# An mLSTM cell and a gated feed-forward layer on one core: the second chunk's query load, scores and values are issued earlier

## The chip, the cores and the metric

The kernel runs on one core of a Trainium2 chip. The metric is the device time of one execution in microseconds (us), the median of the runs shown.

## The reference

The first part is an mLSTM cell over 768 time steps, for 4 batches and 8 heads of 40 features. The second part takes its output as 3072 rows of 320 numbers through two weight matrices with a gelu between them. Everything is float32.

```python
for t in range(S):
    m_new = np.maximum(f_gate[:, :, t] + m, i_gate[:, :, t])
    f_stab = np.exp(f_gate[:, :, t] + m - m_new)
    i_stab = np.exp(i_gate[:, :, t] - m_new)
    C = f_stab * C + i_stab * np.einsum('bhd,bhe->bhde', vt, kt)
    n = f_stab * n + i_stab * kt
    h_tilde = np.einsum('bhde,bhe->bhd', C, qt)
    denom = np.maximum(np.abs(np.einsum('bhd,bhd->bh', n, qt)), 1.0)
    y[:, :, t] = sigmoid(o_gate) * h_tilde / denom
h = x @ w_in                      # (3072, 320) @ (320, 2048)
g = h * sigmoid(1.702 * h)
out = g @ w_out                   # (3072, 2048) @ (2048, 320)
```

## The kernel before

The time axis is cut into six chunks of 128 steps (`w` = 0 to 5; `NW`, `L`). Inside a chunk the recurrence is done in matrix form: scores (keys by queries) times decay weights, times values, plus the queries by the state carried in from the chunk before. All 32 heads of a chunk are worked on; for chunks from the second on, in two halves of 16 heads (`c` = 0, 1).

There is no scheduler at work: the order in which the Python code calls the engines is the order of each engine's queue. The main loop runs over the chunks. For chunk `w` it first makes the product with `w_in` and the gelu (`up` in chunk 0, `up_fast` and `up_strips` later; eight steps `j`), and then the product with `w_out` (`down` in chunk 0), cut into blocks. Between the blocks stand pieces of the attention of chunk `w + 1`: `attention(w + 1)` returns a table `side` of what follows which block, by the list `at`. When the blocks are done, chunk `w + 1`'s first product needs that attention's output, transposed and split (`x_high`, `x_diff` and others).

In chunk 0 `down` is called for 16 blocks: batch `b` 0 to 3, four pieces `n` of the inner dimension, first pieces 0 and 1 of all batches, then 2 and 3. A block is four float32 products of 128 x 320, each of them two rows in the trace (L973). Block `i` stands in the order (b, n) = (0,0) (0,1) (1,0) (1,1) (2,0) (2,1) (3,0) (3,1) (0,2) (0,3) (1,2) and so on.

The steps for the second chunk (`w` = 1) that the change touches:

- `load_squares(1, "q")` (L112 to L116) loads the queries by two DMAs on SP's queue into `q_sq`, in a form from which VectorE can transpose blocks of 32 features. `fill_squares(q_sq)` (L118 to L122) moves the last 8 of the 40 features to their own rows, two copies on ScalarE. `block_transposes(1, n)` for odd `n` (L417 to L421) makes `qT` from it, four transposes on VectorE.
- `load(1, "v")` (L134), the weight pieces (`fetch`, L181) and the decay weights' rows (`spread`, L430) are on the same SP queue.
- `convert(n)` turns a piece of the weights from its bits into numbers: `convert_begin` on ScalarE (L257, L261), `convert_end` on VectorE (L273, L278, L284, L285). Pieces 10 to 19 are `w_out`; 17, 18 and 19 are converted amid the blocks.
- `weights_exp(1, c)` (L469) makes the decay weights of half `c`, 16 exponentials on ScalarE; `weights_mask(1, c)` (L476) zeroes what lies in the future, two instructions on GpSimd. `weights(1, c)` is both.
- `carry(1, c)` (L639) makes the next states' additions, in a pair of PSUM banks for each half; VectorE adds them to the states (L648, with L616 between).
- `scores(1, c)` (L496), in the same two bank pairs; VectorE multiplies them with the weights (L499).
- `values(1, c)` (L540 and L548), with both bank pairs for each half; VectorE reads them (L554, L555) and makes the output `y` (L515).
- `seam_out`, `seam_in` and `seam_turn` bring `y` through DRAM into `xT` (L593, L602, L609); `split_x` and others (L795, L803) make the operands of L857, the next product.
- `weight_sums(n)` (L986), `keep_w01` (L1053) and `split_high`, `split_rest` (L736, L760) prepare weights for later chunks.

`banks()` hands out the two bank pairs in turn.

`count(n)` puts `n` increments of a semaphore, on which nothing waits, into TensorE's queue, as long as some are left of `COUNTS[w]`; chunk 0 has 54 of them.

Of the kernel before, what the change touches and what calls it, by code (L numbers as in the profile page):

```python
# [35 lines left out]
def kernel(  # L36
# [214 lines left out]
    def convert_begin(n):  # L251
        convert_high(n)
        convert_low(n)
# [9 lines left out]
    def convert_end(n):  # L263
        convert_mid(n)
        convert_add(n)
# [353 lines left out]
    def scale(w, c, part=0, parts=1):  # L619
        n = PH // parts  # L620
        hs = slice(c * PH + part * n, c * PH + (part + 1) * n)
        if part == 0:
            vw[w, c] = work.tile([L, PH, D1], FP, tag="u", name="vw")
        e = cols[w][:, 2 * BH + hs.start:2 * BH + hs.stop].unsqueeze(2).to_broadcast([L, n, D1])
        G.tensor_tensor(out=vw[w, c][:, part * n:(part + 1) * n], in0=v_st[:, hs, :], in1=e, op=OP.mult)  # L625
# [85 lines left out]
    def count(n):  # L711
        for _ in range(min(n, left[0])):
            T.sem_inc(steps[at_w[0]], 1)
            left[0] -= 1
# [249 lines left out]
                                   op0=OP.mult, op1=OP.add)  # L964

    def down(w, b, n):
        if n == b == 0:
            left[0], at_w[0] = COUNTS[0], 0
        if n == 0:
            o_ps[w, b] = ps_m.tile([128, DM], FP, tag="m", name="p_out")  # L970
        po = o_ps[w, b]
        for f in range(n * 4, n * 4 + 4):
            T.matmul(po, gs[w, f // 2][:, f % 2, b * L:(b + 1) * L], w_out_sb[f // NH][:, f % NH, :], start=(f == 0),  # L973
                     stop=(f == NF - 1))
            count(1)
        if n == NF // 4 - 1:
            o = op.tile([128, DM], FP, tag="o", name="o_sb")
            A.copy(out=o, in_=po)
            nc.sync.dma_start(out=out[b * S + w * L:b * S + (w + 1) * L, :], in_=o)
# [186 lines left out]
    fetched = {0: range(10, 13), 1: range(13, 18), 3: (18, 19)}  # L1166

    def attention(w):
        at = (0, 1, 3, 3, 5, 6, 8, 8, 9, 11, 12, 13) if w == 1 else (0, 0, 1, 3, 2, 4, 5, 6, 6, 9, 10, 11)
        calls = [[(columns, w)][w == 1:] + [(scale, w, 0), (scale, w, 1), (decay, w, 0, 0), (decay, w, 1, 0)],  # L1170
                 [(weights_mask if w == 1 else weights, w, 0)], [(weights, w, 1)], [(carry, w, 0), (carry, w, 1)], [(open_gates, w)],
                 [(scores, w, 0), (scores, w, 1)], [(values, w, 0)], [(seam_out, w, 0), (seam_in, w, 0)],
                 [(values, w, 1), (seam_out, w, 1), (seam_in, w, 1)], [(seam_turn, w, 0), (split_x, w, 0)], [(split_first, w), (seam_turn, w, 1), (split_x, w, 1)], [(split_on, w)]]
        if w == 1:
            calls[2:4] = [], calls[3] + [(weight_sums, 0)] + calls[2]
        side = {}
        for i, c in zip(at, calls):
            side.setdefault(i, []).extend(c)
        return side

    for w in range(NW):
        more = w + 1 < NW
        if w == 0:
            for j in range(NF // 2):
                if j % 2 == 0:
                    ahead, behind = converted[j // 2]
                    if j:
                        run([(convert, p) for p in ahead])
                    run([(fetch, p) for p in fetched.get(j // 2, ())])
                    up(w, j, lambda: run([(columns_turn, 1) if p is None else (convert, p) for p in behind]), last_seam)  # L1190
                if j == 6:
                    load(1, "o")
                if j == 1:
                    wait_for(w_in[1][:, 1, :])
                    scale(0, 1)
                    load(1, "v")
                if j < B and j % 2:
                    carry(0, j // 2)
                if j == 3:
                    masks()  # L1200
                    gates(1)
                    gates_out(1)
                    columns_in(1)
                if j == 4:
                    spread(1)
                    load_squares(1, "q")
                if j >= B:
                    transposes(1, j - B)
        else:
            if w == 1:  # L1210
                split_diff(1)
# [91 lines left out]
        for i, block in enumerate(blocks):  # L1303
            if w == 0 and i == 0:
                columns(1)
                convert_begin(17)
                weights_exp(1, 0)
                fill_squares(q_sq)
                convert_end(17)
                for n in (1, 3, 5, 7):  # L1310
                    block_transposes(1, n)
            if w == 0 and i in (4, 5):
                convert(14 + i)
            if w + 2 < NW and i == (6 if w == 0 else 0):
                load_gates(w + 2)
            if w == 0 and i == 13:
# [6 lines left out]
            run(side.get(i, []))  # L1323
            if w == 1 and i == 4:
                last_sums(1, 0, (2, 3))
            if w == 0 and i == 5:
                keep_w01()
                wait_for(w_out_flat[1][:, 4 * 512:])
                weight_sums(1)
                weight_sums(3)  # L1330
            if w == 0 and i == 5:
                split_high(0)
                split_rest()
                split_high(1)
# [57 lines left out]
```

## Time and profile before

| | |
|---|---|
| Time, median of 3 runs | 441.79 us (441.62 to 443.78) |
| The profiled execution's own time | 440.54 us |
| Its span, from the first to the last instruction | 438.8 us |
| Granted TensorE clock over the span | 0.999 |
| Blocks of chunk 0 with the second chunk's attention, up to the next product | 64.9 to 108.8 us: 43.9 us |

The lines of the profile are read thus. PE is TensorE's matmuls, PEld its weight loads, DVE is VectorE, ACT ScalarE, POOL GpSimd, SP SyncE; a q behind a name is that engine's queue while it issues a DMA or waits. In the chain that ended last, each line has a start in us, a length in us, the engine, what is written, and the line of the code. In a timeline the line ends, where there was any, with the idle time of the engine before it and who ended it. "issue" is time in which the engine waited for nothing that the profile shows.

### The profile page before, as it was taken

Reading aid. Unit: us, or ns where it says so; the run is one execution under the profiler, and the core shown is the slowest. Engines: PE = TensorE matmul, PEld = TensorE weight load, DVE = VectorE, ACT = ScalarE, POOL = GpSimd, SP = SyncE. Lnnn points to the kernel's source line nnn. Section 1 sums busy time; section 2 is a strip of 40 time slices with the busy share of each in tenths; the row PEclk is TensorE's granted clock in tenths of the full one; section 3 lists DMA queues with packets and bytes.
Section 4 is the critical chain, followed back from the end, with each engine's and each line's share of the span. In section 5 each row is a group of like instructions: output and inputs, shape, how many; then the busy total and the mean of one; then the engine's idle time right before and its main releaser. Section 6 shows DMA issues by size and latency. Waiting matters only on the chain.

```text
span 438.8 us, 13442 instructions
## 1 busy us (share of the span) xinstructions
PE 431.4 (98%) x5342; PEld 373.4 (85%) x5342; DVE 355.6 (81%) x691; ACT 245.3 (56%) x538; POOL 143.4 (33%) x149
## 2 busy tenths in 40 slices
PE   8999999999999999999999999999999999999996
PEld 6877886776888999788999888999887999888996
DVE  5888998979989789759789759789759759779990
ACT  5686779902777900387900386900287930298720
POOL 6501427540056802035712035622036624013100
PEclk9999999999999999999999999999999999999999
DMA  8999999217797525998505997605999605920000
GB/s 168 189 285 215 241 240 219 69 38 181 199 204 153 126 56 153 281 181 150 82 23 133 299 206 148 94 19 133 288 210 154 93 18 133 299 96 2 1 31 30
DMA packets 130733, 64.07 MB, mean 146 GB/s; under 512 B 102208, under 2 KB 122672, under 8 KB 130672
## 3 DMA queue, kind: packets, MB, share of 16 engines
q1 hardware_dynamic: 121232, 57.48, 59.0%
q10 hardware_dynamic: 8768, 4.28, 3.4%
q0 software_dynamic: 672, 1.46, 1.3%
q8 instruction: 43, 0.70, 0.7%
q14 instruction: 18, 0.15, 0.1%
HBM read 51.86 MB, written 11.34 MB: 144 GB/s over the span
## 4 chain that ended last, share of the span: by engine, by line
PE 87%; SPq 4%; DVE 4%; DMA 3%; issue 1%; ACT 1%; DVEq 0%
PE p_out L1027 25%; PE p_h L903 13%; PE p L903 10%; PE p_h L663 7%; PE p L1102 6%; PE p_out L973 5%; PE p L857 3%; SPq L136 3%; PE p_h L857 3%; PE p L923 3%; PE p L540 2%; PE p L496 2%; PE p L548 2%; PE p L639 2%; PE p_h L672 2%; DMA bits<-in_moe_w_in_dram 1%
## 5 line engine op out<-in xcount | busy, mean ns | idle before, releaser
L795 ACT ACTIVATE x_high<-xT 128x512 fp32r<-128x512 f32 x10 | 6.3, 631 | 90.8 <-DVE xT L609 90.8
L1027 PE MATMUL p_out<-w_out,g 128*128 128x160 f32 x384 | 55.5, 301 | 0.0
L1027 PEld LDWEIGHTS p_out<-w_out,g 128*128 128x128 f32 x384 | 52.9, 190 | 1.6 <-ACT g L958 1.3
L835 ACT ACTIVATE g<-g 128x512 f32<-128x512 f32 x80 | 45.7, 629 | 1.8 <-DVE g L963 1.6
L995 POOL TENSOR_TENSOR g<-g 128x512 f32<-128x512 f32 x16 | 20.6, 1306 | 70.8 <-ACT g L835 63.7
L963 DVE SCALAR_TENSOR_TENSOR g<-p,g 128x512 f32<-128x512 f32 x40 | 25.7, 683 | 20.2 <-PE p L903 18.2
L958 ACT ACTIVATE g<-p 128x512 f32<-128x512 f32 x40 | 21.7, 596 | 33.8 <-PE p L903 28.9
L469 ACT ACTIVATE wt<-wt,cols 128x64 f32<-128x64 f32 x160 | 38.9, 335 | 0.1
L1027 PE MATMUL p_out<-t_sb,s 128*128 128x160 f32 x256 | 37.8, 301 | 0.0
L1027 PEld LDWEIGHTS p_out<-t_sb,s 128*128 128x128 f32 x256 | 35.5, 190 | 0.2
L973 PE MATMUL p_out<-w_out,g 128*128 128x320 f32 x128 | 35.7, 436 | 0.0
L963 DVE SCALAR_TENSOR_TENSOR g<-p_h,g 128x512 f32<-128x512 f32 x40 | 25.7, 686 | 11.9 <-PE p_h L903 11.9
L973 PEld LDWEIGHTS p_out<-w_out,g 128*128 128x128 f32 x128 | 23.9, 190 | 9.6
L1012 POOL TENSOR_TENSOR s<-g,s 128x256 f32<-128x256 f32 x16 | 12.9, 831 | 55.2 <-PE p_out L1027 55.2
L663 PE MATMUL p_h<-xT,w_in 128*128 128x256 f32 x128 | 29.8, 385 | 0.6 <-ACT xT L580 0.6
L663 PEld LDWEIGHTS p_h<-xT,w_in 128*128 128x128 f32 x128 | 23.6, 190 | 5.9 <-issue 2.2
L958 ACT ACTIVATE g<-p_h 128x512 f32<-128x512 f32 x40 | 21.6, 593 | 10.3 <-PE p_h L903 9.2
L476 POOL TENSOR_SCALAR_AFFINE_SELECT wt<-wt 64x1024 f32<-64x1024 f32 x20 | 24.3, 1215 | 6.9 <-ACT wt L469 6.1
L625 POOL TENSOR_TENSOR vw<-v_st,cols 128x656 f32<-128x656 f32 (+1 forms) x13 | 16.7, 1298 | 26.1 <-PE p_out L1027 15.4
L1032 DVE TENSOR_TENSOR o_sb<-o_sb,p_out 128x160 f32<-128x160 f32 x56 | 16.3, 314 | 9.8 <-PE p_out L1027 9.3
L1102 PE MATMUL p<-w_part,g_part 128*128 128x320 f32 x128 | 24.0, 309 | 0.0
L421 DVE STREAM_TRANSPOSE qT<-q_sq 128x512 f32<-128x512 f32 x20 | 20.3, 1106 | 1.3 <-ACT q_sq L122 1.3
(255 smaller groups left out, 1085.9 us busy)
## 6 DMA issues: line engine op xcount, KB each, us to landing
w_diff<-w_row SPq DMA_DIRECT2D x16, 512.0 KB, 4.8
wt<-m_row SPq DMA_DIRECT2D x20, 256.0 KB, 6.1
bits<-in_moe_w_in_dram SPq DMA_DIRECT2D x8, 512.0 KB, 7.6
w_low<-w_row SPq DMA_DIRECT2D x8, 512.0 KB, 6.0
out_dram<-o_sb SPq DMA_DIRECT2D x24, 160.0 KB, 2.5
q_sq<-in_q_dram SPq DMA_DIRECT2D x10, 320.0 KB, 7.1
eo<-in_o_gate_dram SPq DMA_DIRECT2D x5, 640.0 KB, 7.2
bits<-in_moe_w_out_dram SPq DMA_DIRECT2D x8, 320.0 KB, 6.1
```

The lines of the kernel that those rows point to most:

```text
L469: A.activation(out=x[:, h, :], in_=x[:, h, :], func=AF.Exp, scale=-1.0, bias=cols[w][:, c * PH + h:c * PH + h + 1])
L476: G.affine_select(out=r, in_=r, compare_op=OP.is_ge, fill=0.0, base=0, pattern=[[0, PH], [1, HL]], channel_multiplier=-1)
L663: T.matmul(ph[j][i][:, t], w_in[f // 4][:, c, f % 4 * 128:f % 4 * 128 + 128], x[:, c, t], start=(first and c == 0 and n == 0), stop=(not f ...
L835: A.activation(out=g, in_=g, func=AF.Gelu_apprx_sigmoid)
L857: T.matmul(dst[i], a(i), x, start=(first and m == which[0]), stop=(last and m == which[-1]))
L903: mm = T.matmul(to[f], a(f)[r], x[r], start=(first and n == 0), stop=(last and n + 1 == len(parts)))
L958: A.activation(out=g[:, i, :], in_=opened[w, j][0][i], func=AF.Copy, scale=-BASE)
L963: V.scalar_tensor_tensor(out=g[:, i, :], in0=opened[w, j][1][i], scalar=1.0 + 1.0 / BASE, in1=g[:, i, :], op0=OP.mult, op1=OP.add)
L973: T.matmul(po, gs[w, f // 2][:, f % 2, b * L:(b + 1) * L], w_out_sb[f // NH][:, f % NH, :], start=(f == 0), stop=(f == NF - 1))
L995: G.tensor_tensor(out=a10, in0=a00, in1=a10, op=OP.subtract)
L1027: T.matmul(po, a(f), b[:, f, :], start=(f == 0), stop=(f == NH - 1))
L1102: T.matmul(dst, g_part[n, b, f // 2][:, f % 2], wo[n, f][0][:, wo[n, f][1]], start=(f == order[0] and n < 2), stop=(f == order[-1] and n > 0))
```

## The change

Queue orders change in chunk 0's two products; the program has the same instructions, but for where the semaphore increments stand.

- The load of the second chunk's queries goes from step `j` = 4 of the first product to `j` = 1, ahead of the values' load, and their feature move from the start of the blocks to step `j` = 5.
- Before the blocks, the first half's exponentials come ahead of the conversion of piece 17, and the queries' transposes ahead of its part on VectorE. Pieces 18 and 19 are converted ahead of blocks 5 and 6, not 4 and 5.
- The second half's weights come after block 1, not in the list after the carry; the sum `weight_sums(0)` stays after the carry.
- Scores come after block 4 (before: 6), the first values after block 6 (8), the second after block 7 (9). The steps of the seam and the split behind them come one block earlier. `open_gates` stays after block 5, and the carry after block 3.
- `keep_w01`, two weight sums and the first splits of `w_in` go from block 5 to block 6.
- The 54 increments begin at block 10 instead of block 0, three after each product instead of one.

```diff
     def down(w, b, n):
-        if n == b == 0:
+        if b == 1 and n == 2:
             left[0], at_w[0] = COUNTS[0], 0
...
-            count(1)
+            count(3)
...
     def attention(w):
-        at = (0, 1, 3, 3, 5, 6, 8, 8, 9, 11, 12, 13) if w == 1 else (0, 0, 1, 3, 2, 4, 5, 6, 6, 9, 10, 11)
+        at = (0, 1, 1, 3, 5, 4, 6, 6, 7, 10, 11, 12) if w == 1 else (0, 0, 1, 3, 2, 4, 5, 6, 6, 9, 10, 11)
...
         if w == 1:
-            calls[2:4] = [], calls[3] + [(weight_sums, 0)] + calls[2]
+            calls[3] += [(weight_sums, 0)]
...
                     scale(0, 1)
+                    load_squares(1, "q")
                     load(1, "v")
...
                     spread(1)
-                    load_squares(1, "q")
                 if j >= B:
                     transposes(1, j - B)
+                if j == 5:
+                    fill_squares(q_sq)
...
             if w == 0 and i == 0:
                 columns(1)
+                weights_exp(1, 0)
                 convert_begin(17)
-                weights_exp(1, 0)
-                fill_squares(q_sq)
-                convert_end(17)
                 for n in (1, 3, 5, 7):
                     block_transposes(1, n)
-            if w == 0 and i in (4, 5):
-                convert(14 + i)
+                convert_end(17)
+            if w == 0 and i in (5, 6):
+                convert(13 + i)
...
-            if w == 0 and i == 5:
+            if w == 0 and i == 6:
                 keep_w01()
...
-            if w == 0 and i == 5:
+            if w == 0 and i == 6:
                 split_high(0)
```

## The prediction

> **What bounds the kernel now.** I read the page's table of busy times first, then the chain that ended last, then TensorE's waits in the stretch that the change touches (60 to 112 us: the product with `w_out` of the first chunk, with the attention of the second chunk between its blocks).
>
> ```profile
> PE 431.4 (98%) x5342; PEld 373.4 (85%) x5342; DVE 355.6 (81%) x691; ACT 245.3 (56%) x538; POOL 143.4 (33%) x149
> ```
> ```profile
> PE p L639 <- issue: 0.5, 1, 0.5
> PE p L857 <- ACT x_high L795: 0.4, 1, 0.4
> ```
>
> TensorE is busy 98% of the span, and in this stretch it waits twice: 0.47 us in the middle of the carry (L639), with nothing that it waits for, and 0.41 us for x_high at the end. The granted clock is 1.00 in every window here. So the change can only remove these two waits, or add others. The chain in time shows both, and where scores and values stand:
>
> ```profile
> 65.04 8.62 PE p_out L973 x32
> 73.66 1.11 PE p L639 x89
> 74.76 0.47 issue
> 75.23 0.52 PE p L639 x32
> 75.75 6.66 PE p_out L973 x24
> 82.41 2.02 PE p L496 x128
> 84.43 4.50 PE p_out L973 x16
> 88.94 1.07 PE p L540 x64
> 90.01 0.93 PE p L548 x64
> 90.94 2.35 PE p_out L973 x8
> 93.29 1.07 PE p L540 x64
> 94.37 0.98 PE p L548 x62
> ```
>
> A block is 8 rows of L973, 2.2 us. From 95.4 the chain leaves TensorE and goes through VectorE and the seam to x_high, but TensorE has its 48 remaining rows of L973 (13.2 us) beside that and is short of work by 0.41 us only. Shortening that chain by 4 us is therefore worth 0.4 us.
>
> **Part one: blocks, scores and values.** The same 64 block products, 128 carry, 128 score and 256 value instructions run, in another order: scores after block 4 instead of 6, values after blocks 6 and 7 instead of 8 and 9, eight blocks behind them instead of six. TensorE's own sum is unchanged. The second values end two blocks earlier, 4.5 us less what is lost before them; the seam (99.4 to 108.4 now) moves with them, while TensorE ends its blocks at about the old time. The wait of 0.41 us goes: -0.4. The cover is then some 3 us deep; ScalarE's four store issues of the second seam (99.03 to 102.27) and its copies of p_out move along and stay ahead of their readers.
>
> The price is what scores need. TensorE will reach them at 75.75 + 2.22 = 78.0 instead of 82.4. They use the two bank pairs that the carry filled, and VectorE must have added those to the states first:
>
> ```profile
> 73.27 1.26 ACT L122 COPY q_sq<-q_sq 32x512 f32<-32x512 f32 x2
> 74.55 3.94 ACT L469 ACTIVATE wt<-wt,cols 128x64 f32<-128x64 f32 x16
> ```
> ```profile
> 74.56 3.97 DVE L421 STREAM_TRANSPOSE qT<-q_sq 128x512 f32<-128x512 f32 x4 [1.25 <-ACT q_sq L122]
> 78.36 0.51 DVE L648 TENSOR_TENSOR state_mid<-p,state_mid 128x328 f32<-128x328 f32 x1
> 78.90 1.22 DVE L616 TENSOR_TENSOR state<-state_mid,cols 128x328 f32<-128x328 f32 x1
> 80.15 0.50 DVE L648 TENSOR_TENSOR state<-p,state 128x328 f32<-128x328 f32 x1
> ```
>
> Today the first pair is free at 80.6 and the second at 82.1: scores start just behind. After the change VectorE transposes the queries at once (68.1 to 72.1), since their feature move is long done. Then it stands at the conversion of piece 17, which ScalarE now starts only behind the first sixteen exponentials. Those begin when ScalarE is through with the columns (68.2) and the weights' rows have landed. The rows for the first half landed at 66.6; with the query load ahead of them they come later by 1.5 us (320 KB at the 211 GB/s of this stretch) to 3.4 us (what the two query loads took: last weights' row landed at 68.6, second query load at 72.0). So they begin between 68.2 and 70.0; I take 69.1. Then 3.9 us of exponentials and 1.1 of conversion (L257 and L261) give 74.2. VectorE's last two steps of the conversion are 0.74 + 0.69, to 75.6; beside GpSimd's work they took 1.27 + 1.02 now, to 76.5. The first pair's adds are 0.51 + 0.50 + 0.50, or with a slow L616 as above 2.23: the pair is free between 77.1 and 78.7, and the second 1.5 us later. TensorE wants them at 78.0 and 79.0. Bounds: 0 with the early figures, 2.0 us with the late ones all together (second pair free at 81.0, scores ended at 82.0 instead of 80.0). I take 0.5.
>
> **Code of TensorE.** The stop of 0.47 us has no releaser. The page's queue q8 (instruction) has 43 packets, 0.70 MB, so 16 KB each, for about 11,300 TensorE instructions: 262 per packet. The packet before the stop started at 72.61 and took 1.11; TensorE went on at 75.23, 1.5 us after its end. In calm stretches a packet starts when TensorE is some 300 instructions short of the first use; that place was passed at 64.5, and the DMA engines were full until 75. [...] I therefore read the stop as late code. The carry keeps its place, so the stop stays (0.47; between 0 and 1.9, as the DMA backlog at 64.5 goes).
>
> What moves is the next border. The count steps (semaphore increments, 54 in all) stand beside the first 54 block products now, and in the changed kernel only from block 10 on, three to a product, so scores come 60 instructions earlier in the stream (28 steps, and 8 products of 4 instructions). The border that fell 132 instructions into the scores (at 83.4, with code there since 80) falls 192 into them, 1.5 us after their start: 79.5. The packet that brings it started at 77.27 and ended at 78.55; plus 1.5 it is there at 80.05. That is a stop of 0.55, if nothing else has held the scores; it overlaps with the wait for the bank pairs, so together I take 1.0, with bounds 0 and 2.0. The second border of this kind lies in the second values: the call comes at about 86.1, the code 3.6 to 5.0 us later, the use at 90.7: 0 to 0.5, taken as 0.2. The three-fold steps themselves cost nothing: a step takes 0.05, a block product 0.54, and TensorE's sequencer runs ahead of it.
>
> [...]
>
> **Part two: the query load.** SP issues its two DMAs (0.6 and 0.5 us) ahead of the values' load at 43.6 instead of at 60.87, past 3 value loads, 12 weight pieces and 4 weights' rows, all of which land 1.5 to 3.4 us later. Values are read at 67.8 (landed 52.1): nothing. Pieces 13 to 16 landed between 53.6 and 61.1 and are converted from 55.7, 60.7, 61.9 and 63.0: piece 16 may hold ScalarE by up to 1.5 us, hidden by TensorE, which reads these weights only from block 8 on. The feature move (2 copies, 1.26 us) goes to about 56, where ScalarE now idles 2.72 us until 59.73; without that cover it would hold the gelu by 1.26. What is left is the later weights' rows, counted above.
>
> **Part three: masks, conversions, sums.** GpSimd's second mask comes ahead of the first weight sum: it ends at about 80.5 instead of 81.1, before the product with the scores (L499) is free to run. The conversions of pieces 18 and 19 (4.4 us on VectorE) follow L499 instead of preceding it: L499 ends at about 82.5, they end at 86.9, and the first values' adds (L554) want VectorE at about 87.5. Weight sums and the `w_out` store move one block later on an idle GpSimd. All this is covered by 0.6 us, which is thin: the adds free the bank pairs for the second values.
>
> **Sum.** -0.4 + 1.0 + 0.2 = +0.8 on the profiled execution: 440.54 (span 438.8 and 1.7 around it) to 441.3. That execution lies 1.25 below the median of 441.79, so on the median's scale 442.6.
>
> **The rivals.** *All covers hold:* bank pairs free in time and no late code, the old stop too gone: -0.4 - 0.5, 440.9. For it: VectorE needs only the short durations; against: the DMA engines are full until 75. *Code never holds TensorE:* the stop at 74.76 has another cause and stays; what is left is -0.4 + 0.5 for the bank pairs, 441.9. *Slower (the other side):* the query load ahead of the weights' rows makes ScalarE's two runs of exponentials the bound. It decides from the point where the first exponentials begin later than about 69.5: second mask at 81.7, scores late by 2.0, L499 ending at 83.2, conversions at 87.6, and the adds of the first values then hold the banks of the second by up to 1. With -0.4 and 0.2: +2.8, 444.6. For it: the query load's own 3.4 us; against: that time was measured with the queue full of other work. That the change doesn't bring the values earlier at all is the end of this rival, not a case by itself.
>
> **How the numbers follow.** Forecast 0.48, code never holds 0.17, all covers hold 0.15, slower 0.20. The measurement can tell about 0.5%, 2.2 us, from no change. Faster than that would need more than the two waits hold; I leave 0.04 for what the trace doesn't show. Above 444.0 lies the slower rival and little of the forecast: 0.18. The range, 440.8 to 444.8, takes in the end where all covers hold and most of the slower rival.
>
> **What would show it.** In the trace after: no wait of L857 for x_high; the stop in L639 still there; a wait of L496 for VectorE's L648, or an issue stop inside L496, of 0.5 to 1 us; the copies of L122 at about 56; the first L469 at 69 or later; the second L548 ending near 92.5. The forecast is wrong if L496 starts at 78.0 and runs 2.0 us, or if a wait over 1.5 us stands ahead of scores or values.

## The result, and the profile after

| | before | after |
|---|---|---|
| Time, median of 21 executions each | 441.65 us (439.17 to 444.61) | 447.82 us (441.62 to 453.27) |
| Ratio after to before | | 1.0088, interval 1.0062 to 1.0115 |
| The profiled execution's own time, and its span | 440.54, 438.8 us | 444.1, 442.4 us |

The change made the kernel slower. The ratio leaves out the nine slowest executions of the changed kernel, those over 1.5% above its fastest, so it is smaller than the quotient of the two medians (1.014).

The first reading is not of a line of the profile but of the granted TensorE clock of each execution. Before, it was 0.998 or more in 70 of the 74 executions that stand beside the experiments below. After:

| Mean granted clock | Executions | Time, us |
|---|---|---|
| 0.998 or more | 3 | 441.6 to 444.1 |
| 0.994 to 0.996 | 4 | 444.7 to 445.2 |
| 0.989 to 0.992 | 10 | 445.7 to 452.1 |
| 0.988 or less | 4 | 450.3 to 453.3 |

The profiled execution is one of the first row, so its profile shows the waits, but not what they usually set off. TensorE's busy time, then its waits from 60 to 115 us and from 110 to 140 us:

```profile
PE 432.1 (98%) x5342; PEld 373.7 (84%) x5342; DVE 358.3 (81%) x691; ACT 245.4 (55%) x538; POOL 142.8 (32%) x149
```
```profile
PE p L496 <- DVE state L648: 1.5, 2, 1.2
```
```profile
PE p L857 <- ACT g L958: 1.6, 1, 1.6
```

The two old waits (L639 for nothing shown, L857 for x_high) are gone. In their place scores wait 1.5 us for the carry's banks, and the next product has a new wait of 1.65 at 132. In this execution the span is 3.6 us longer than before: the blocks begin 0.6 later (65.47 instead of 64.88; the full clock had begun 1.1 later), from there to the next product it takes 44.4 us instead of 43.95, and from there to the end 332.5 instead of 330.0. So the stage that the change rearranges lost 0.45 us here, and most of the rest is the wait at 132 and one of 0.6 at 383, of L923 for VectorE. The chain behind the first wait, on ScalarE and then on VectorE:

```profile
56.47 1.25 ACT L122 COPY q_sq<-q_sq 32x512 f32<-32x512 f32 x2
59.51 0.69 ACT L257 ACTIVATE w_out<-bits 128x512 f32<-128x512 f32 x1 [1.78 <-DMA bits<-in_moe_w_out_dram]
64.39 0.69 ACT L257 ACTIVATE w_out<-bits 128x512 f32<-128x512 f32 x1 [0.38 <-DMA bits<-in_moe_w_out_dram]
69.61 3.93 ACT L469 ACTIVATE wt<-wt,cols 128x64 f32<-128x64 f32 x16
73.45 0.65 ACT L257 ACTIVATE w_out<-t_sb 128x512 f32<-128x512 f32 x1
```
```profile
69.12 3.98 DVE L421 STREAM_TRANSPOSE qT<-q_sq 128x512 f32<-128x512 f32 x4
74.13 0.91 DVE L273 TENSOR_SCALAR w_out<-w_out 128x512 f32<-128x512 f32 x1 [1.03 <-ACT w_out L257]
77.61 0.49 DVE L648 TENSOR_TENSOR state_mid<-p,state_mid 128x328 f32<-128x328 f32 x1
78.68 0.50 DVE L648 TENSOR_TENSOR state<-p,state 128x328 f32<-128x328 f32 x1
80.15 0.50 DVE L648 TENSOR_TENSOR state<-p,state 128x328 f32<-128x328 f32 x1
88.68 0.83 DVE L554 TENSOR_TENSOR u<-p,cols 128x656 f32<-128x656 f32 x1
90.42 1.49 DVE L506 TENSOR_SCALAR den<-u 128x16 f32<-128x16 f32 x1
92.33 3.23 DVE L510 SCALAR_TENSOR_TENSOR eo<-eo,u 128x640 f32<-128x640 f32 x1
96.41 0.83 DVE L554 TENSOR_TENSOR u<-p,cols 128x656 f32<-128x656 f32 x1
```

ScalarE now waits for weight pieces (DMA bits), which it did not before: 1.78 us for piece 13 and 0.38 for piece 16. VectorE waits 1.03 for ScalarE's part of piece 17 and begins L648 at 77.61. The first bank pair is free at 79.18 and the second at 80.65; TensorE is at the scores at 78.0. And the second half's L554 begins at 96.41, though its products end two blocks earlier: L506 and L510 of the first half take 1.49 and 3.23 us. Before, the same lines were:

```profile
92.77 0.17 DVE L506 TENSOR_SCALAR den<-u 128x16 f32<-128x16 f32 x1
93.36 0.76 DVE L510 SCALAR_TENSOR_TENSOR eo<-eo,u 128x640 f32<-128x640 f32 x1
95.37 0.84 DVE L554 TENSOR_TENSOR u<-p,cols 128x656 f32<-128x656 f32 x1 [0.32 <-PE p L548]
```

GpSimd's weight sums ran beside them (after: from 88.97, 5.92 us; before they had ended at 92.67). So the seam is 1.0 us later than before (the blocks began 0.6 later), not 4 earlier.

The wait at 132, on ScalarE and on TensorE:

```profile
129.87 0.37 ACTq L749 DMA_DIRECT2D w_row<-w_diff  x1
130.33 1.05 ACT L753 CAST w_low<-w_low 128x1024 fp32r<-128x1024 f32 x1 [4.48 <-DMA w_row<-w_diff]
132.69 1.08 ACT L958 ACTIVATE g<-p 128x512 f32<-128x512 f32 x2
```
```profile
133.83 0.73 PE L857 MATMUL p<-x_rest,w_rest 128*128 128x512 f32 x2 [1.65 <-ACT g L958]
```

ScalarE stands 4.48 us at the issue of the fourth store of `w_diff`, until the third has landed (129.79). In both traces the DMAs of SP and ScalarE take eight completion semaphores in turn (104, 106, 108 to 113), in the order of the program, and of the 301 issues in each none stands before the last DMA on its semaphore has landed (the closest 0.02 us behind). The changed order of the DMAs in the blocks puts the fourth store on 112, that of the third; before it had 106, last used by an m_row store that had landed at 119.98. The store was issued at 124.09 then.

### The profile page after: what moved, and what is told of

Its sections match the earlier page's. It is cut to its first block, busy times and chain, and to the rows that moved or that the text cites. A ratio compares the mean times of both kernels' runs of the same rounds, so it can differ in the third digit from the quotient of the medians.

```text
span 442.4 us, 13440 instructions
## 1 busy us (share of the span) xinstructions
PE 432.1 (98%) x5342; PEld 373.7 (84%) x5342; DVE 358.3 (81%) x691; ACT 245.4 (55%) x538; POOL 142.8 (32%) x149
## 5 line engine op out<-in xcount | busy, mean ns | idle before, releaser
L958 ACT ACTIVATE g<-p 128x512 f32<-128x512 f32 x40 | 21.7, 596 | 32.3 <-PE p L903 29.1
L469 ACT ACTIVATE wt<-wt,cols 128x64 f32<-128x64 f32 x160 | 38.9, 335 | 0.1
L973 PE MATMUL p_out<-w_out,g 128*128 128x320 f32 x128 | 35.7, 436 | 0.0
L973 PEld LDWEIGHTS p_out<-w_out,g 128*128 128x128 f32 x128 | 23.9, 190 | 9.6
L958 ACT ACTIVATE g<-p_h 128x512 f32<-128x512 f32 x40 | 21.6, 593 | 9.9 <-PE p_h L903 9.1
L625 POOL TENSOR_TENSOR vw<-v_st,cols 128x656 f32<-128x656 f32 (+1 forms) x13 | 16.3, 1267 | 24.2 <-ACT cols L393 12.7
```

Source lines behind the costliest of these rows:

```text
L469: A.activation(out=x[:, h, :], in_=x[:, h, :], func=AF.Exp, scale=-1.0, bias=cols[w][:, c * PH + h:c * PH + h + 1])
L958: A.activation(out=g[:, i, :], in_=opened[w, j][0][i], func=AF.Copy, scale=-BASE)
```

## The experiments

Three theories. *Bank*: VectorE frees the carry's banks too late for the earlier scores. *Slot*: the store's semaphore. *Late code*: the prediction's code terms. All ratios are to the kernel before, on the same chip.

### The changed kernel, and each theory's part alone

**e1_after**, the changed kernel with no edit.

> The changed kernel again, beside the others on the same chip. Both theories: 444 to 450 us, 1 to 2% over the kernel before, with a granted clock of 0.985 to 1.0 that differs between executions. Slot theory (the fourth store of w_diff on ScalarE, L749, waits for the semaphore slot of the store before it, and everything behind it on ScalarE waits too): ScalarE idle for over 4 us behind that store, TensorE waiting about 1.6 us or more in L857 for ScalarE's L958. Bank theory (scores wait for VectorE's carry adds): L496 waits 1 to 2 us for L648, and that is the larger part of the loss.

445.46, ratio 1.0114 (1.0061 to 1.0166). This profiled execution (446.7 us, clock 0.991) shows what the first did not. Scores, and then, for two stretches, busy time of PE, PEld, DVE, ACT and POOL with the granted clock behind them (then the DMA share and GB/s):

```profile
80.73 1.18 PE L496 MATMUL p<-qT,kT 40*64 40x64 f32 x64 [2.31 <-DVE state L648]
82.21 1.99 PE L496 MATMUL p<-qT,kT 40*64 40x64 f32 x64 [0.30 <-DVE state L648]
```
```profile
75.00:80.00 5.00, 3.42 (x115) 2.39 (x102) 4.24 (x6) 5.00 (x20) 2.36 (x2) 1.00 0.70 100
82.00:88.00 6.00, 5.79 (x71) 4.32 (x72) 4.80 (x8) 5.92 (x8) 4.37 (x3) 0.50 0.18 50
```

Behind a wait of 2.3 us the granted clock was 0.5 from 81.75 for 6.83 us: the second 64 score products take 1.99 us instead of 1.16. L857 starts 5.4 us later than before; the blocks had begun 1.0 later.

**e2_keep_pool**: the fourth store from GpSimd.

```diff
-                        keep(w_diff_row, 3, w_diff[1, 3])
+                        keep(w_diff_row, 3, w_diff[1, 3], G)
```

> The changed kernel, with the fourth store of w_diff issued by GpSimd, where it doesn't wait for that slot. Slot theory: the wait of L857 for L958 is gone and the time falls to 441 to 443 us, within 0.5% of the kernel before, with the clock at 0.997 or more in every execution. Bank theory: the wait of L496 is unchanged, and the time stays at 444 us or more.

445.34, ratio 1.0132 (1.0087 to 1.0178). L857 no longer waits for L958 (profiled 442.2, clock 1.0, scores waited 0.7). The median did not move, so the slot is not the main loss. With four executions on each side, spread over 4 to 5 us, a part of 1 us would not show.

**e3_before_wait**: the kernel before, with a small extra store on ScalarE that waits until the third one has landed.

```diff
+                        nc.scalar.dma_start(out=w_diff_row[2][:, 0:8],
+                                            in_=w_diff[1, 2].rearrange("p c m -> p (c m)")[:, 0:8].bitcast(FP))
                         keep(w_diff_row, 3, w_diff[1, 3])
```

> The kernel before, with a small store on ScalarE ahead of the fourth store of w_diff that must wait until the third has landed; all else as before. Slot theory: ScalarE idles some 4 us until that landing (about 128 us), L857 waits 1 us or more for L958, and the time rises to 444 us or more, with a lower clock in some executions. Bank theory: within 1 us of the kernel before, plus at most the 1.6 us of that wait.

445.43, ratio 1.0117 (1.0089 to 1.0146). From the first L857 to the end it takes 334.5 us instead of 330.0, with one wait of 2.25 us:

```profile
133.16 0.73 PE L857 MATMUL p<-x_rest,w_rest 128*128 128x512 f32 x2 [2.25 <-ACT g L958]
134.26 1.05 PE L857 MATMUL p<-x_rest,w_rest 128*128 128x512 f32 x2
```

A pair takes 0.62 us at full clock; here 1.05, with the clock at 0.5 from 134.07 for 3.41 us.

**e4_load_early**: the kernel before with the query load and the feature move early, and nothing else.

```diff
+                    load_squares(1, "q")
                     load(1, "v")
...
                     spread(1)
-                    load_squares(1, "q")
...
+                if j == 5:
+                    fill_squares(q_sq)
...
-                fill_squares(q_sq)
```

> The kernel before, with only the query load and the feature move early (part two of the prediction); blocks, scores, values and count steps as before. Slot theory: the stores of w_diff keep their slots, so 441 to 442.5 us, no more than 0.2% over the kernel before. A third theory, that the later weights' rows and pieces cost the time: 444 us or more, with TensorE waiting in L496 or in the blocks.

443.12, ratio 1.0049 (1.0020 to 1.0078). ScalarE waited 3.84 us for a weight piece, its exponentials began 7.0 us behind the first block product (before: 4.4), and scores, though in their old place, waited 0.8. So the load alone costs.

**e10_at_only**: the kernel before with only the places changed.

```diff
-        at = (0, 1, 3, 3, 5, 6, 8, 8, 9, 11, 12, 13) if w == 1 else ...
+        at = (0, 1, 3, 3, 5, 4, 6, 6, 7, 10, 11, 12) if w == 1 else ...
```

> The kernel before with only the list of places changed: scores after block 4, values after 6 and 7, seam and split one block earlier; query load, conversions, masks and counts as before. Bank theory: the adds of the carry end where they did (80.6 for the first pair, 82.1 for the second), TensorE wants them at 78 and 79, so L496 waits 2.5 to 3.5 us, the clock halves in some of the executions, and with the fourth store's slot shifted as in the changed kernel (L857 waits 1 to 2 us for L958) the median is 446 to 450, above the changed kernel's or level with it. If the other edits are what costs, the median is under 444.

449.31, ratio 1.0156 (1.0071 to 1.0240), as the bank theory had it. Its waits, 20 to 115 and 115 to 145 us:

```profile
PE p L496 <- DVE state L648: 2.0, 1, 2.0
PE p L639 <- issue: 1.0, 1, 1.0
```
```profile
PE p L857 <- ACT g L958: 2.3, 1, 2.3
```

The clock was halved behind both waits of 2 us. Whether the other edits of the change soften this can't be told, since the intervals overlap; they do not pay for it.

**e9_at_old** and **e14_at_old_conv**: the changed kernel with the places undone; in the second also pieces 18 and 19 ahead of blocks 4 and 5 again.

```diff
-        at = (0, 1, 1, 3, 5, 4, 6, 6, 7, 10, 11, 12) if w == 1 else ...
+        at = (0, 1, 1, 3, 5, 6, 8, 8, 9, 11, 12, 13) if w == 1 else ...
...                                        (second kernel only)
-            if w == 0 and i in (5, 6):
-                convert(13 + i)
+            if w == 0 and i in (4, 5):
+                convert(14 + i)
```

> The changed kernel with one part undone: scores, values, seam and split again after the blocks of before (scores after 6, values after 8 and 9); the query load, the conversions' order, the masks and the counts stay as changed. Its DMA instructions fall on the same semaphores as before. Bank theory: VectorE's adds of the carry end near 81 to 82 as in the changed kernel, but TensorE wants the banks only at 82.4, so L496 waits 0.5 us or less, no other wait is over 1 us, clock 0.998 or more. Slot theory: no wait of L857 for L958. Both together: median 440.5 to 442.5, within 0.4% of before. If the early query load or the later conversion costs by itself, the median stays above 443.

> The changed kernel with the places of scores and values as before, and the conversions of pieces 18 and 19 ahead of blocks 4 and 5 as before, so that they no longer stand between the late scores and L499. What is left of the change is the early query load with its feature move, the first exponentials ahead of the conversion of piece 17, the second mask and the counts. If VectorE's order behind the scores was what was left in the kernel with the places undone: no wait of L540 for L499, clock 0.998 or more in most executions, median 440.5 to 442.5. If the early query load costs by itself (as in the kernel of before with that load alone, 443.1), it stays at 442.5 to 444.

444.54, ratio 1.0041 (0.9996 to 1.0087), and 444.35, ratio 1.0077 (1.0040 to 1.0113). No scores' wait in either profile, but a mean clock under 0.998 in 11 of the 20 executions, which neither profile caught. The interval of the first takes in 1. In the second the values still waited 1.2 us for L499. The first one's profiled 444.69 says little of the change: its full clock began only 18.8 us after the start of the span (4.4 to 11.0 in the other profiles), and the blocks at 69.7, 4.8 us later than before. Both ratios overlap with e4's: what is left fits the early query load, and the conversions' places make no difference that these intervals show.

**e8_count_old**: the increments as before.

```diff
-        if b == 1 and n == 2:
+        if n == b == 0:
...
-            count(3)
+            count(1)
```

> The changed kernel with the semaphore increments of TensorE as before: one behind each product from block 0 on, instead of three behind each from block 10 on. Late-code theory (the place of the borders between code packets in the stream decides): scores come 28 instructions later in the stream and values too, stops with no releaser appear or go by 0.5 to 1.0 us, and the time moves by up to 1 us against the changed kernel. Bank and slot theory: L496 waits 1.2 to 2.6 us for L648 as in the changed kernel, and the median stays within 1.5 us of it, 444 to 448.

447.8, ratio 1.0128 (1.0092 to 1.0164): as the changed kernel. The stop in the carry came back at 0.2 us, with its code packet starting at 73.21 again (66.50 after, 72.61 before). So the increments can move that border, though they alone don't decide: e4 has the old ones, its packet started at 67.19, and there was no stop. It is worth 0.2 to 1.0 us (e8, e10). No stop of this kind was seen in scores or values, if the values' waits put down to "issue" further below are waits for banks, as read there.

### What makes the banks late

**e7_load_late**: the query load late again, its feature move behind the first exponentials, ahead of piece 17.

```diff
-                    load_squares(1, "q")
                     load(1, "v")
...
                     spread(1)
+                    load_squares(1, "q")
...
-                if j == 5:
-                    fill_squares(q_sq)
...
                 weights_exp(1, 0)
+                fill_squares(q_sq)
                 convert_begin(17)
```

> The changed kernel with the query load back where it was (step 4 of the first product) and its feature move back at the head of the blocks, between the first sixteen exponentials and the conversion of piece 17. Bank theory: the weights' rows land earlier again and the exponentials begin near 68.3, but VectorE's transposes of the queries wait for the feature move (about 73.5) and end near 77.5, the conversion stands behind them, L648 begins at 79 or later: L496 waits 2.5 us or more, the clock halves there, median 446 to 449. If the early query load itself is what costs (traffic, slots, later rows), the median is under the changed kernel's by 1 us or more, 441 to 444.

451.39, ratio 1.0253 (1.0199 to 1.0308). Scores wait 8.6 us in all and the clock is halved for 13.65 us:

```profile
76.60 3.86 DVE L421 STREAM_TRANSPOSE qT<-q_sq 128x512 f32<-128x512 f32 x4 [7.95 <-ACT q_sq L122]
```
```profile
85.34 1.99 PE L496 MATMUL p<-qT,kT 40*64 40x64 f32 x64 [7.47 <-DVE state L648]
```

The query load landed at 75.9. With the scores this early, a late load is far worse than an early one.

**e17_rows_pool** and **e18_conv_first_rows**: the four rows of decay weights on GpSimd's queue, and the store too; in the second also ScalarE's part of piece 17 ahead of the exponentials.

```diff
-                nc.sync.dma_start(out=x[n * HL:(n + 1) * HL].rearrange("s j i t -> s (j i t)"),
+                (G if w == 1 else nc.sync).dma_start(out=x[n * HL:(n + 1) * HL].rearrange("s j i t -> s (j i t)"),
```

> The changed kernel with the fourth store of w_diff on GpSimd's queue (as in the kernel with that edit alone) and, besides, the second chunk's four rows of decay weights (spread) loaded by GpSimd's queue instead of SP's, where they stand behind the query load, the values' load and sixteen weight pieces. Theory: it is the landing of these rows, 1 to 8 us after TensorE's first block product, that sets the first exponentials, the conversion of piece 17, L648, and so the scores' wait. Then the rows land by 64 to 66 in every execution, the exponentials begin at the columns' end, 3.3 us behind the first block product, L496 waits 0.3 to 1.5 us, and the clock halves seldom: median 441.5 to 443.5, 2 to 4 us under that kernel's 445.3. If the rows' landing is not what sets it, L496 waits 2 us or more as before and the median stays at 444.5 to 447.

> The kernel with ScalarE's part of the conversion of piece 17 ahead of the exponentials and the store on GpSimd's queue, and the four rows of decay weights loaded by GpSimd's queue besides. Rows theory: the exponentials begin 4.4 us behind the first block product in every execution, L648 begins near 75.5, L496 waits 0.3 us or less; what is left is the second L540's wait for the first half's L555 (0.5 to 1.6 us, behind the conversions of pieces 18 and 19). Median 441.5 to 443.5, no lower than before, since TensorE's waits of before were 0.9 us together. If the rows are not the cause, the median stays at that kernel's 445.

449.3, ratio 1.0209 (1.0175 to 1.0243), and 449.95, ratio 1.0185 (1.0142 to 1.0228). The theory that the rows' landing is what sets the exponentials falls, and the profile of the first says what does:

```profile
67.51 0.67 ACT L257 ACTIVATE w_out<-bits 128x512 f32<-128x512 f32 x1 [3.35 <-DMA bits<-in_moe_w_out_dram]
72.69 3.93 ACT L469 ACTIVATE wt<-wt,cols 128x64 f32<-128x64 f32 x16
```
```profile
82.30 3.69 PE L496 MATMUL p<-qT,kT 40*64 40x64 f32 x128 [4.19 <-DVE state L648]
```

The rows had landed by 67.7 (first half); ScalarE stood at the conversion of piece 16, which the rows had now pushed back. Behind that conversion in ScalarE's queue come the gelu, the kT copies, the columns, the exponentials and piece 17. In the second kernel ScalarE waited 9.6 us for pieces, 6.1 of it for piece 16; the columns came late, GpSimd's L625 behind them too, and the carry itself waited 4.0 us for that. Put together over the profiles with the order of the changed kernel on ScalarE (all counted from the first L973, us; scores stand after block 6 in e9 and e14, 5 in e11 and e15, else 4):

| Kernel | ScalarE waits for pieces | first L469 | first L648 | L496 waits | clock halved there |
|---|---|---|---|---|---|
| e8 | 0 | 3.3 | 11.3 | 0.3 | no |
| e2 | 0 | 3.3 | 11.3 | 0.7 | no |
| e9 | 0 | 3.3 | 11.3 | none | no |
| e11 | 1.9 | 3.8 | 11.8 | none | no |
| after | 2.2 | 4.1 | 12.1 | 1.5 | no |
| e14 | 2.6 | 5.0 | 13.0 | none | no |
| e1 | 3.1 | 5.3 | 13.3 | 2.6 | 6.8 us |
| e13 | 4.8 | 6.9 | 14.9 | 4.0 | 6.8 us |
| e15 | 5.4 | 8.1 | 16.1 | 3.0 | 6.8 us |
| e17 | 6.0 | 8.0 | 16.0 | 4.2 | 10.2 us |

ScalarE has 1.3 us to spare (it idles that long in e2, e8 and e9); what the waits take beyond it comes out in L469 to 0.2 us: 6.0 - 1.3 = 4.7, and 8.0 - 3.3 = 4.7. Only e14 and e15 are 0.4 and 0.8 later than that; there the exponentials waited for the rows as well, 0.3 and 0.7 us. L648 begins 8.0 us behind L469 in all ten. With the query load behind the rows ScalarE waited not at all in the kernel before, e3 and e10, and 1.7 us in e7.

### Taking the bank wait away

**e5_conv_later** and **e6_conv_later_pool**: piece 17 converted ahead of block 4; in the second also the store from GpSimd.

```diff
-                convert_begin(17)
...
-                convert_end(17)
-            if w == 0 and i in (5, 6):
+            if w == 0 and i in (4, 5, 6):
                 convert(13 + i)
```

> The changed kernel with the conversion of piece 17 (its part on ScalarE and its part on VectorE) moved from the head of the blocks to ahead of block 4; all else as changed, the fourth store of w_diff still on ScalarE's queue. Bank theory (the loss is the scores' wait for L648, because VectorE's adds of the carry stand behind that conversion, and the granted clock halves after a wait of some 2 us): L648 begins near 74.5 instead of 77.6 to 79.1, L496 waits for it 0.5 us or less, the granted clock of the span is 0.998 or more, and the median falls by 2 to 4 us against the changed kernel, to 441.5 to 443.5, with the wait of L857 for L958 (1.6) left. Slot theory alone (the loss is the store's wait ahead of L958): the median stays at 444.5 to 447, however short L496's wait is. Late code alone: TensorE stops with no releaser in or near L496, 0.5 us or more, in spite of free banks.

> As the kernel with the later conversion, and the fourth store of w_diff issued from GpSimd's queue besides. Bank and slot theory together: no wait of L857 for L958, L496 waits 0.5 us or less, clock 0.998 or more, median 439.5 to 441.5: at the kernel before or up to 1 us under it, since the two waits of 0.47 and 0.41 us of before are gone as well. If a third cause is at work (the blocks' own order, the load ahead of the weights' rows by itself), it stays above 442.5.

447.69, ratio 1.0139 (1.0103 to 1.0176), and 445.07, ratio 1.0102 (1.0084 to 1.0120). The scores' wait was gone in both, and the time was not. In e6 the wait went to the values, and the clock was halved there for 6.83 us:

```profile
80.97 3.44 DVE L284 TENSOR_SCALAR t_sb<-t_sb 128x512 uint16<-128x512 uint16 x1
85.05 2.35 DVE L499 TENSOR_TENSOR wt<-p,wt 128x1024 f32<-128x1024 f32 x2
```
```profile
PE p L540 <- DVE wt L499: 2.6, 1, 2.6
```

The conversion now stands ahead of L499, and its L284 takes 3.44 us beside a weight sum instead of 0.73. In e5 the first values waited 1.4 us for L499, and the second 2.5 us put down to "issue"; these began at 93.22, just as VectorE's L555 had ended (92.27 + 0.84), so I read it as a bank again. The clock stayed full there.

**e11_at_one_pool**: the changed kernel with scores after block 5, values after 7 and 8, and the store from GpSimd.

```diff
-        at = (0, 1, 1, 3, 5, 4, 6, 6, 7, 10, 11, 12) if w == 1 else ...
+        at = (0, 1, 1, 3, 5, 5, 7, 7, 8, 10, 11, 12) if w == 1 else ...
```

> The changed kernel with scores, values and seam only one block earlier than before (scores after block 5, values after 7 and 8) and the fourth store of w_diff issued by GpSimd. Bank theory: TensorE wants the banks at about 80.2 and 81.2; VectorE frees them at 79 to 81.5: L496 waits 0.3 us or less in most executions, no wait of L857 for L958, median 440.5 to 442.5. If there is a further cost in VectorE's order (conversions of pieces 18 and 19 behind L499), a wait of L540 of 0.5 to 1.5 us is left and the median is 442.5 to 444.

445.73, ratio 1.0085 (1.0056 to 1.0115). No scores' wait, clock 0.998 or more in 7 of 10 executions; but L857 waited 1.8 us for x_high, with L506 at 1.48 and L510 at 3.24. Those seven took 443.5 to 446.2, so a loss of some 2 to 5 us needs no half clock.

**e12_conv_first_pool**: ScalarE's part of piece 17 ahead of the exponentials, and the store from GpSimd.

```diff
-                weights_exp(1, 0)
                 convert_begin(17)
+                weights_exp(1, 0)
```

> The changed kernel with ScalarE's part of the conversion of piece 17 again ahead of the first sixteen exponentials, and the fourth store of w_diff issued by GpSimd. VectorE's part then follows the transposes of the queries at once: L648 begins at about 76.2 instead of 77.6 to 79.1. Bank theory: L496 waits 0.5 us or less; the second mask comes 1.2 us later, at about 81.5, and L499 ends near 83.5; no wait of L857 for L958; median 441 to 443. If removing the scores' wait only moves it to the values, as in the two kernels with the conversion ahead of block 4, L540 waits 1 us or more for L499 and the median is 443.5 to 446.

445.21, ratio 1.0054 (1.0015 to 1.0094), the lowest ratio with the places as changed, though its interval overlaps with the changed kernel's. L496 waited 0.3; the second L540 began 0.1 us behind the end of L555 (90.78 + 0.84), which frees its bank:

```profile
91.73 1.20 PE L540 MATMUL p<-v_st,wt 64*64 64x41 f32 x61 [1.55 <-issue]
```

**e13_sums_late** and **e15_one_sums_pool**: the two weight sums wait for the second half's outputs, in the changed kernel and (with `i == 9`) in that of e11.

```diff
             if w == 0 and i == 6:
                 keep_w01()
-                wait_for(w_out_flat[1][:, 4 * 512:])
+            if w == 0 and i == 8:
+                wait_for(ys[1, 1][:, 1, 0:DM])
                 weight_sums(1)
                 weight_sums(3)
```

> The changed kernel with GpSimd's two weight sums (L986, 5.9 us together) made to wait until the outputs of the second half are written; nothing else. Theory of VectorE's slow steps (beside GpSimd's sums L506 takes 1.5 us instead of 0.2 and L510 3.2 instead of 0.8, so the first half's output ends 3.8 us later): L506 takes 0.2, L510 0.8, the second L554 begins at 93 instead of 96.4, the first L739 at 96 to 97 instead of 100.4, and the seam's operands come 3 us earlier. TensorE did not wait for them in the changed kernel, and the scores' wait and the store's wait stay, so the median moves by less than 1.5 us: 444 to 448. If the outputs were what held TensorE, it falls to 441 to 443.

> The kernel with scores and values one block earlier and the store on GpSimd's queue, and GpSimd's two weight sums made to wait for the outputs of the second half. There L857 waited 1.8 us for x_high because L506 and L510 ran beside those sums. Theory of the slow steps: L506 0.2, L510 0.8, the second L554 near 94, no wait of L857 for x_high, median 1.5 to 3 us under that kernel's 445.7: 442.5 to 444. If the wait for x_high has another cause (the seam's stores), it stays at 1 us or more and the median does not move.

448.93, ratio 1.0149 (1.0079 to 1.0219), and 450.88, ratio 1.0196 (1.0135 to 1.0257). L506 takes 0.17 and L510 0.76 in both, as expected, so the sums are what slowed them. But L857 still waited for x_high, 1.3 and 3.4 us: the late sums now ran beside L765 and L766, which took 3.80 us each instead of 1.22, with the seam's transposes (L609) behind them on VectorE. And the times rose: in both profiles scores waited 3 to 4 us, behind ScalarE's waits for pieces (4.8 and 5.4 us).

**e16_spread_sums_pool**: all of it at once. Pieces 17 and 18 behind L499, VectorE's part of piece 19 behind the first L555, the sums late, the store from GpSimd.

```diff
-                convert_begin(17)
...
-                convert_end(17)
             if w == 0 and i in (5, 6):
-                convert(13 + i)
+                convert(12 + i)
+            if w == 0 and i == 6:
+                convert_begin(19)
...
         V.tensor_tensor(out=v, in0=view(po), in1=v, op=OP.add)
+        if w == 1 and c == 0:
+            convert_end(19)
         outputs(w, hs, u)
```

> The changed kernel with each of the waits found so far taken away: conversions of pieces 17 and 18 behind L499 instead of ahead of L648 and L554, that of piece 19 behind the first L555, the two weight sums behind the second half's outputs, the fourth store of w_diff on GpSimd's queue. If VectorE's order is the whole cause: L648 begins near 74.5, L496 waits 0.3 us or less, L540 waits 0.5 us or less for L499 or L555, no wait of L857, median 440 to 442, level with before or up to 1 us under it. If something else of the change costs (the early query load, the later exponentials by the second mask), a wait of L540 for L499 of 1 us or more is left and the median is 443 to 445.

447.12, ratio 1.0117 (1.0070 to 1.0164). No scores' wait and none for L499, but the second values waited 2.0 us for the first L555 (88.66 + 0.84; they began at 89.61), and the clock was halved from 90.30 for 6.83 us. In e5, e12, e16 and e18 alike, the values that waited for "issue" began 0.10 to 0.11 us behind the end of L555; on that rests the reading as a bank. No version here beats the kernel before.

## Why the prediction was wrong

**The step that failed first: the delay of the weight pieces.** Part two has the transfers behind the query load "land 1.5 to 3.4 us later", and says that "piece 16 may hold ScalarE by up to 1.5 us, hidden by TensorE". In the profiled execution piece 13 landed at 59.44 instead of 53.59, 5.9 us later, and held ScalarE for 1.78 us, piece 16 for 0.38. The lower bound counted 320 KB; the query load is two DMAs of 320 KB, and 640 KB at the same 211 GB/s make 3.1 us. The upper bound was short too: SP stood 5.5 us in one issue of the values' load (before: 3.0), and issued piece 13 by 3.5 to 4.1 us later. And "hidden by TensorE" named who reads the piece, not what is queued behind its conversion. Behind it on ScalarE stand the columns, the exponentials and piece 17, hence L648 and the scores. The waits for pieces were 0 to 5.4 us in one and the same order on ScalarE (table above; 6.0 in e17, with the rows on another queue), and e1 had 3.1 where the same kernel's first profile had 2.2.

**The term that was mis-sized: scores waiting for banks, 0.5 with bounds 0 to 2.0.** It was 1.5 in the profiled execution, 0.3 to 2.6 in e8, e2 and e1, and 4.0 in e13. Where ScalarE waited for no piece (e2, e8) it was 0.7 and 0.3, as forecast. For the first pair the working gave 77.1 to 78.7, and 79.2 was measured, with the blocks 0.6 later; but that execution was a middling one. The working also left out the first two steps of VectorE's part of piece 17 (L273, L278), which took 0.91 and 1.25 us while GpSimd's mask ran: from L469 to L648 it had 6.5 to 7.4 us, and 8.0 was measured.

**The term that was missing: the clock.** A wait of 2 us or more was counted at its own length. In 13 of the 15 cases profiled it came with 3.41 to 13.65 us at half clock; by estimate up to half of that, 1.7 to 6.8 us, is lost. 18 of the 21 executions have a clock under 0.998, and their times rise as it falls. It is not the whole spread from 441.6 to 453.3: within one row of the table the times still differ by up to 6.4 us, which no profile here explains. The prediction read "1.00 in every window" as a property of the kernel; in that profile no wait of this stage was longer than 0.5 us.

**The gain did not exist as costed.** The wait for x_high did go in the profiled execution, but not because the seam "moves with them": the second L554 came 1.0 us later than before, and x_high was ready at 109.82 instead of 108.77. TensorE, itself 1.0 us later, came at 109.87. The move brought L506 and L510 beside GpSimd's sums (+1.3 and +2.5 us). VectorE had idled 2.24 us for the first values before, and L506 began at 92.77, when the sums had ended; it idles no more there.

**What came near by luck.** In the profiled execution the stage lost 0.45 us, where the sum had 0.8. That is no support for the sum: the bank wait was 1.0 larger, the stop in the carry, which the sum kept, went (0.47), and the two code terms (0.7) did not come.

**The DMA order.** It was said of the query load which transfers land later, not that DMAs change semaphores. That gave the 1.65 us at 132, about twice the 0.88 us that could be gained at all. How much of the median it makes is open: e3 shows what such a wait can cost alone, but e2, without it, is no faster than e1.

**Code.** The stop in the carry was said to stay; it went, with the increments (e8 brings 0.2 of it back). No run shows the two code terms, 0.5 and 0.2, and the places of the borders in scores and values were an estimate: where scores or values waited, it was for VectorE, or for "issue" until 0.10 to 0.11 us behind the end of L555, read here as a bank. In the carry there were stops of 1.0 in e3 and e10. That the earlier values end near 92.5 was right (92.7), as was L122 at 56 (56.47) and L469 at 69 or later (69.61).

**The rivals.** The slower one named the mechanism: query load ahead, ScalarE late, "later than about 69.5". Its way went through the pieces rather than the rows, and its price of 2.8 was short by the clock. "All covers hold" fell; its condition, no wait at scores with the places as changed, was met only in kernels where the wait came up at the values instead. "Code never holds TensorE" was right of scores and values, but not of the time: it kept 0.5 for the banks and the old stop. The sign named for a wrong forecast, a wait over 1.5 us ahead of scores, stood just at its limit in the profiled execution (1.21 + 0.31) and was passed in e1 (2.6).

**What is left open.** e9 and e14 have a mean clock under 0.998 in 11 of their 20 executions, and their one profile each shows no halved stretch; which wait sets it off there was not seen. Of the changed kernel itself two executions were profiled; where the slowest ones lost their time is inferred from the others.

## What to carry to other kernels

Before a step is brought forward on the engine that is 98% busy, list what the engines that feed it have still to do by then, in their queue order: here VectorE had idled 2.24 us ahead of the first values' read, and each rearrangement tried only moved the wait to another product. When a load goes ahead in a shared queue, follow the transfers it delays to the first instruction that waits for them, and count everything queued behind that instruction. And count a TensorE wait of 2 us as 4 to 5 in a kernel like this one, an estimate: in e3 a wait of 2.25 us with 3.41 us of half clock made 4.5, in e10 one of 2.0 had 6.83 us of half clock behind it.

## What the runs showed of the hardware

**The clock.** In the profiles here 15 waits of TensorE between 60 and 140 us were 2.0 us or longer (1.98 the shortest); with 13 of them the clock went to 0.5, beginning inside the wait or within 1.2 us of its end, for 3.41 (e3), 6.83 (e1), 10.24 (e17) or 13.65 us (e7). The shortest, 1.98 us in e16, had 6.83 us of it. The two others were 2.2 (e13) and 2.5 us (e5). Behind none of 1.8 us (e7, e11) or less did it begin.

**VectorE beside GpSimd.** L510 took 3.23 us instead of 0.76 while L986 ran, and L506 1.49 instead of 0.17; L506 ended at 91.91 and L510 at 95.56, while the two sums ended at 91.9 and 94.9. In e13 and e15, with the sums later, L765 took 3.80 beside them instead of 1.22. L554 and L555, which read PSUM and one more operand, kept their 0.83 and 0.84. Why some instructions took longer beside the sums and others did not is not shown.

**Completion semaphores.** A DMA's issue can wait for a transfer whose landing it needs only for the semaphore that they share: before, the fourth store was issued at 124.09, 3.9 us ahead of the third's landing; after, it was issued at 129.87, behind the third's landing at 129.79. ScalarE's next work stood with it, 4.48 us here.
